# Columns of a weight used chunk by chunk: `w_val` laid out in four chunks of 128 output columns, and the steps of the program written in another order

## The chip, the cores and the metric

The kernel runs on one core of one Trainium2 chip. The metric is device microseconds (us) of one execution, as the median of several runs. One further execution was profiled, and the views below come from it.

TensorE (PE) does the matmuls, VectorE (DVE), ScalarE (ACT) and GpSimd (POOL) the elementwise work, and SyncE (SP) issues the DMAs. PEld is TensorE's loading of weights.

## The reference, cut to what matters

```python
B, H, S, Ns, D = 8, 8, 512, 32, 64              # all float32
scores = x @ state.T / sqrt(D)                  # per batch and head: [512, 32]
xread  = softmax(scores) @ state                # tokens read the state
scores2 = state @ x.T / sqrt(D)
sread  = softmax(scores2) @ x                   # the state reads the tokens
y = concat([xread, sread], axis=2)              # [B, H, 544, 64] -> x: [B, 544, 512]

gate = sigmoid(causal convolution of x over tokens, 5 taps, one weight per channel)
val  = x @ w_val                                # 512 x 512
out  = (gate * val) @ w_out                     # 512 x 512, out: [8, 544, 512]
```

Since `xread` is a product of probabilities and the state, `xread @ w_val` is computed as probabilities times (`state @ w_val`). The 512 token rows of each batch go through the batch loop; the 32 state rows of all batches are gathered and done once, in a tail.

## The kernel before, in words

**The work of a batch.** Eight batches, and per batch a chain: `load_xT` and `load_x` fetch the tokens; `scores` (tile `sc`) multiplies them with the scaled state `ss`; the softmax over the state runs as `mx` (maximum), `sl` (scores less maximum), `ex` (exponential), `sm` (sum, then a small number is added by `guard`), `rc` (its reciprocal), `ex` times `rc`, and the transposes by `probs` into `a`; the softmax over the tokens runs as `nb`, `e2`, `sum2`, `r2`, and the transposed exponentials (`e2p`, copied to `e2T`) multiply `x` in `state_read` (`srp`), whose result goes by `sr` and the transpose `srT` to the tail's rows. `state_val` multiplies the state with `w_val` (`sgv`); a scaling writes it as `sw0` for batch 0 and as `swh` with a rest `swl` for the others. `read` gives `xr`, the gate's taps follow (`acc`, `last`), and `sig` is the gate. `values` (`val`) multiplies `a` with the scaled `sgv`: two matmuls of plain f32 for each of four column chunks of batch 0, six matmuls of split numbers for the others. `gated` gives `g`, which is split into `gh` and `gl`, `project` (`op`) multiplies by `w_out` in twelve matmuls for each of four token tiles, and `o` is stored.

**Batch 0 is done otherwise in two ways.** Its scores and its first softmax are done in two halves of the tokens, as `xT` comes in two loads; and its taps are folded into the read: `z5` is the state times the five taps (`tap_state`, on POOL), and `read_conv` accumulates five shifted reads in `xr`, so that `gate_read` (L528) makes `sig` of `xr` directly.

**The weights.** `w_val` and `w_out` reach the core as 64-bit numbers, each 128 rows of 512 (one chunk, 512 KB) in one load (`vw`, `ow`). A chunk is turned into f32 by four steps: `wc` on ScalarE (L305), its clamp on POOL or VectorE (L320), `wp` on ScalarE (L313) or VectorE, and the join on VectorE (L325), which for `w_val` writes its part of `wv`. Chunks are rows of `w_val`, that is input channels, and `state_val` sums over nothing else: each of the eight matmuls of `state_val` takes 64 of the 512 input channels and all 512 output columns.

**What sets the order.** The program is a list of numbered steps; the string `ORDER` names them one by one in the order in which they are written out, with a letter where a step may run on several engines (`a`, `v`, `g`). Each engine runs its own steps in that order. `PLACES` says which buffer or PSUM bank (`ps0` to `ps7`) each tile takes; a tile that takes the place of another waits until the last reader of that one is done, so a load can be held at SyncE by the buffer that it writes to. `warm_up(i)` is a pair of matmuls whose result nobody reads.

The matmuls that the change divides, as they stand before:

```python
def state_val(b):
    for q in range(SB):
        for g in range(NG):
            h = slice(D * g, D * g + D)
            nc.tensor.matmul(
                get("sgv", b, g)[NS * q:NS * q + NS], su[h, b, q], wv[h, q],
                start=True, stop=True, tile_position=(D * g, NS * q))
```

Of the kernel before, what the change touches and what calls it, by code (L numbers as in the profile page):

```python
# [833 lines left out]
```

## Time and profile before

| | |
|---|---|
| time, median of 3 runs | 214.68 us (214.29 to 215.73) |
| the profiled execution's own time | 213.62 us |
| its span (first to last instruction) | 211.8 us |
| instructions | 4629 |
| TensorE busy | 204.5 us, 97% of the span |
| VectorE, ScalarE, POOL busy | 172.6, 145.2, 148.7 us |
| bytes moved by DMA | 31.25 MB, 148 GB/s over the span |

The span is the profiled part of that execution; its own time holds some 1.8 us more. An engine counts as busy while it executes, and matmuls are pipelined, so a busy TensorE can still be waiting inside. The times in the rows count from the start of the span.

### The profile page before, as it was taken

How to read it: one execution, taken by the hardware profiler on the slowest of the kernel's cores; microseconds unless marked ns; L12 is line 12 of the kernel's file. 1: busy time of each engine (PE TensorE's matmuls, PEld its weight loads, DVE VectorE, ACT ScalarE, POOL GpSimd, SP SyncE). 2: the span in 40 equal slices, each digit the busy share in tenths (PEclk: the TensorE clock that was granted, in tenths of full speed). 3: DMA queues.
4: the chain of work that ended last, by engine and by line, in shares of the span. 5: the costliest groups of instructions: out<-in, count | busy, mean ns of one | idle time of the engine just before them, and what ended most of it. 6: DMA issues, size and time to landing. Idle time of an engine off the chain costs nothing.

```text
span 211.8 us, 4629 instructions
## 1 busy us (share of the span) xinstructions
PE 204.5 (97%) x1791; PEld 149.1 (70%) x1791; DVE 172.6 (81%) x269; ACT 145.2 (69%) x307; POOL 148.7 (70%) x128
## 2 busy tenths in 40 slices
PE   8977999999999999999999999999999999999994
PEld 8754344877588577877686858688866868898883
DVE  1699898999899998999889999969987896697300
ACT  2497999985995889879947983685666573642421
POOL 1179899879989996879987899795859914520200
PEclk9999999999999999999999999999999999999999
DMA  6999970000446885410009960209400400040316
GB/s 167 403 391 377 422 329 6 0 0 3 124 200 226 297 295 162 189 54 0 3 2 325 388 280 3 99 0 288 161 0 3 152 3 0 0 150 3 149 50 198
DMA packets 9364, 31.25 MB, mean 148 GB/s; under 512 B 1130, under 2 KB 1406, under 8 KB 7422
## 3 DMA queue, kind: packets, MB, share of 16 engines
q1 hardware_dynamic: 9342, 30.96, 40.1%
q8 instruction: 14, 0.23, 0.4%
q14 instruction: 8, 0.07, 0.1%
HBM read 22.04 MB, written 8.91 MB: 146 GB/s over the span
## 4 chain that ended last, share of the span: by engine, by line
PE 88%; DVE 3%; POOL 3%; DMA 2%; ACT 1%; issue 0%; SPq 0%; DVEq 0%; POOLq 0%
PE val L560 20%; PE op L568 14%; PE op L569 14%; PE op L570 14%; PE srp L414 4%; PE sgv L369 4%; PE xr L497 3%; PE e2p L404 3%; PE sc L386 3%; PE tval L633 3%; DMA su<-sT 2%; PE xr L512 2%; POOL ex L269 1%; PE top L569 1%; PE top L568 1%; PE top L570 1%
## 5 line engine op out<-in xcount | busy, mean ns | idle before, releaser
L537 DVE SCALAR_TENSOR_TENSOR acc<-xr,cw,acc 128x511 f32<-128x511 f32 (+2 forms) x84 | 59.8, 737 | 4.5 <-ACT last L264 2.2
L568 PE MATMUL op<-woh,gh 128*128 128x512 f32 (+1 forms) x132 | 52.2, 396 | 0.0
L569 PE MATMUL op<-wol,gh 128*128 128x512 f32 (+1 forms) x132 | 51.2, 388 | 0.0
L570 PE MATMUL op<-woh,gl 128*128 128x512 f32 (+1 forms) x132 | 51.0, 387 | 0.0
L269 POOL TENSOR_TENSOR acc<-acc,last 128x508 f32<-128x508 f32 x24 | 31.2, 1301 | 17.3 <-DVE acc L537 11.5
L269 POOL TENSOR_TENSOR gl<-g,gh 128x512 fp32r<-128x512 f32 x28 | 36.9, 1326 | 8.4 <-ACT gh L256 7.5
L568 PEld LDWEIGHTS op<-woh,gh 128*128 128x128 f32 x132 | 24.9, 189 | 6.2 <-ACT o L256 0.8
L570 PEld LDWEIGHTS op<-woh,gl 128*128 128x128 f32 x132 | 24.8, 188 | 5.5
L569 PEld LDWEIGHTS op<-wol,gh 128*128 128x128 f32 x132 | 24.8, 188 | 4.9
L563 DVE SCALAR_TENSOR_TENSOR g<-sig,val 128x512 f32<-128x512 f32 x32 | 21.6, 682 | 7.1 <-PE val L560 3.4
L256 ACT COPY o<-op 128x512 f32<-128x512 f32 (+1 forms) x32 | 18.0, 575 | 10.0 <-PE op L570 8.4
L549 ACT ACTIVATE sig<-acc 128x512 f32<-128x512 f32 x28 | 17.5, 640 | 8.6 <-POOL acc L269 7.9
L532 ACT ACTIVATE acc<-xr,cw 128x512 f32<-128x512 f32 x28 | 19.5, 699 | 5.6 <-PE xr L497 4.2
L560 PE MATMUL val<-ah,swh 128*128 128x512 f32 x56 | 23.1, 412 | 0.0
L560 PE MATMUL val<-ah,swl 128*128 128x512 f32 x56 | 22.1, 394 | 0.0
L560 PE MATMUL val<-al,swh 128*128 128x512 f32 x56 | 22.0, 392 | 0.0
L264 ACT ACTIVATE last<-xr,cw 128x508 f32<-128x508 f32 x23 | 16.0, 696 | 4.8 <-DVE acc L537 3.5
L269 POOL TENSOR_TENSOR sl<-sl,mx 128x1024 f32<-128x1024 f32 (+1 forms) x8 | 14.5, 1811 | 5.1 <-DVE mx L460 5.0
L269 POOL TENSOR_TENSOR al<-sl,ah 128x1024 fp32r<-128x1024 f32 x7 | 16.8, 2399 | 1.5 <-ACT ah L256 1.4
L256 ACT CAST gh<-g 128x512 fp32r<-128x512 f32 x21 | 12.9, 628 | 6.5 <-DVE g L563 6.5
L269 POOL TENSOR_TENSOR ex<-ex,rc 128x1024 f32<-128x1024 f32 (+1 forms) x9 | 15.6, 1728 | 0.4 <-DVE rc L477 0.4
L560 PEld LDWEIGHTS val<-ah,swh 128*128 128x128 f32 x56 | 10.5, 188 | 4.6 <-issue 1.6
(126 smaller groups left out, 389.6 us busy)
## 6 DMA issues: line engine op xcount, KB each, us to landing
x<-x SPq DMA_DIRECT2D x8, 1024.0 KB, 8.6
out<-o SPq DMA_DIRECT2D x31, 256.0 KB, 2.5
xT<-xT SPq DMA_DIRECT2D x7, 1024.0 KB, 5.9
vw<-w_val SPq DMA_DIRECT2D x4, 512.0 KB, 7.2
ow<-w_out SPq DMA_DIRECT2D x4, 512.0 KB, 7.3
xT<-xT SPq DMA_DIRECT2D x2, 512.0 KB, 5.1
su<-sT SPq DMA_DIRECT2D x2, 256.0 KB, 3.8
z<-z SPq DMA_DIRECT2D x2, 256.0 KB, 7.4
```

The lines of the kernel that those rows point to most:

```text
L256: nc.scalar.copy(out, in_)
L264: nc.scalar.mul(out, in_, factor)
L269: (nc.vector if e == "DVE" else nc.gpsimd).tensor_tensor(out, a, b, op=how)
L369: nc.tensor.matmul(get("sgv", b, g)[NS * q:NS * q + NS], su[h, b, q], wv[h, q], start=True, stop=True, tile_position=(D * g, NS * q))
L532: nc.scalar.mul(get("acc", b, pr), pt, cw[:, HALO, pr:pr + 1])
L537: nc.vector.scalar_tensor_tensor(acc[:, d:], get("xr", b, pr)[:, :S - d], cw[:, HALO - d, pr:pr + 1], acc[:, d:], op0=ALU.mult, op1=ALU.add)
L549: nc.scalar.activation(get("sig", b, pr), get("acc", b, pr), AF.Tanh, scale=0.5)
L560: nc.tensor.matmul(get("val", b, k), w, a, start=(i == 0), stop=(i == len(parts) - 1))
L563: nc.vector.scalar_tensor_tensor(get("g", b, k), get("sig", b, k), 1.0, get("val", b, k), op0=ALU.add, op1=ALU.mult)
L568: nc.tensor.matmul(pt, gh, woh[:, k, c], start=(k == 0), stop=False)
L569: nc.tensor.matmul(pt, gh, wol[:, k, c], start=False, stop=False)
L570: nc.tensor.matmul(pt, gl, woh[:, k, c], start=False, stop=(k == NPR - 1))
```

## The change

`w_val` is laid out on the host so that a chunk of 128 rows in memory holds all 512 input channels of 128 output columns. `wv` becomes `[128, chunk, input block, 128]`. `state_val` of batches 1 to 7 reads all chunks with one matmul as before, through another view; that of batch 0 is divided into four parts, `state_val_part(0, k)`, of eight matmuls with 128 columns, and each part has two scalings `state_val_part_high`, of 128 columns each, in place of two of 512. The tail's use of `wv` follows the new shape.

`ORDER` and `PLACES` are replaced as a whole. Of the loads, the state (`su`) and the taps (`cww`) come first, then both halves of batch 0's tokens; which engine does a clamp, a copy, an addition or a split differs in many steps of all batches.

```diff
-        ("ident", [P, P], F32), ("wv", [P, NPR, C], F32), ...
+        ("ident", [P, P], F32), ("wv", [P, NPR, NPR, P], F32), ...
...
+    def columns(k):
+        return wv[:, k].rearrange("p q c -> p (q c)")
+
+    def state_val_part(b, k):
+        for q in range(SB):
+            for g in range(NG):
+                h = slice(D * g, D * g + D)
+                nc.tensor.matmul(
+                    get("sgv", b, g, k)[NS * q:NS * q + NS, :P], su[h, b, q], wv[h, k, q],
+                    start=True, stop=True, tile_position=(D * g, NS * q))
+
+    def state_val_part_high(e, b, g, k):
+        scale(e, get("sw0", b)[:, g, k * P:(k + 1) * P], get("sgv", b, g, k)[:, :P], HALF)
+
     def state_val(b):
...
-                    get("sgv", b, g)[NS * q:NS * q + NS], su[h, b, q], wv[h, q],
+                    get("sgv", b, g)[NS * q:NS * q + NS].rearrange("p (k c) -> p k c", c=P), su[h, b, q], wv[h, :, q],
...
-        op(state_val, b)
-        for g in range(NG):
-            op(state_val_high, b, g)
-            if b > 0:
+        if b > 0:
+            op(state_val, b)
+            for g in range(NG):
+                op(state_val_high, b, g)
                 op(state_val_low, b, g)
+        else:
+            for k in range(NPR):
+                op(state_val_part, b, k)
+                for g in range(NG):
+                    op(state_val_part_high, b, g, k)
...
-    weights(w_val, "vw", "v", lambda k: wv[:, k])
+    weights(w_val, "vw", "v", columns)
...
-        "w_val": np.ascontiguousarray(moe_w_val).view(np.int64),
+        "w_val": np.ascontiguousarray(moe_w_val.reshape(NJ, P, NJ, P).transpose(2, 1, 0, 3)).view(np.int64).reshape(moe_w_val.shape),
```

Two places show how the order moves. A row names the line, the operation and the tiles; `sgv_0_1_3` is the second half (1) of batch 0's (0) part 3. Lines are those of each kernel's own file, so that L369 before answers to L374 and L385 after, and L512 to L528.

VectorE and POOL ahead of batch 0's read. POOL before:

```order
L320 TENSOR_SCALAR wc_v_2_181<-wc_v_2_181 128x512
L320 TENSOR_SCALAR wc_v_3_184<-wc_v_3_184 128x512
L269 TENSOR_TENSOR ex_0_168<-ex_0_168,rc_0_191 128x2x256
L425 TENSOR_SCALAR sm_0_175<-sm_0_175 128x2x8
L269 TENSOR_TENSOR ex_0_168<-ex_0_168,rc_0_191 128x2x256
L269 TENSOR_TENSOR z5_0_260<-z_72,cwb_71 128x640
L320 TENSOR_SCALAR wc_v_1_245<-wc_v_1_245 128x512
```

POOL after:

```order
L322 TENSOR_SCALAR wc_v_1_181<-wc_v_1_181 128x512
L271 TENSOR_TENSOR ex_0_179<-ex_0_179,rc_0_192 128x2x256
L441 TENSOR_SCALAR sm_0_183<-sm_0_183 128x2x8
L271 TENSOR_TENSOR z5_0_261<-z_72,cwb_71 128x640
L271 TENSOR_TENSOR ex_0_179<-ex_0_179,rc_0_192 128x2x256
L322 TENSOR_SCALAR wc_v_3_257<-wc_v_3_257 128x512
L322 TENSOR_SCALAR wc_o_0_259<-wc_o_0_259 128x512
```

`z5` has moved ahead of the second half of `ex`.

VectorE at the same place, before:

```order
L470 TENSOR_REDUCE sm_0_175<-ex_0_168 128x2x8
L325 SCALAR_TENSOR_TENSOR wv_65<-wc_v_3_184,wp_v_3_195 128x512
L477 RECIPROCAL rc_0_191<-sm_0_175 128x2x8
L488 STREAM_TRANSPOSE a0_0_239<-ex_0_168 128x256
L449 STREAM_TRANSPOSE sl_1_242<-sc_1_1_221 128x512
L449 STREAM_TRANSPOSE sl_1_242<-sc_1_0_219 128x512
L488 STREAM_TRANSPOSE a0_0_239<-ex_0_168 128x256 x3
L460 TENSOR_REDUCE mx_1_328<-sl_1_242 128x32
```

and after:

```order
L327 SCALAR_TENSOR_TENSOR wv_65<-wc_v_1_181,wp_v_1_185 128x512
L486 TENSOR_REDUCE sm_0_183<-ex_0_179 128x2x8
L465 STREAM_TRANSPOSE sl_1_221<-sc_1_1_210 128x512
L465 STREAM_TRANSPOSE sl_1_221<-sc_1_0_208 128x512
L493 RECIPROCAL rc_0_192<-sm_0_183 128x2x8
L504 STREAM_TRANSPOSE a0_0_250<-ex_0_179 128x256 x2
L476 TENSOR_REDUCE mx_1_253<-sl_1_221 128x32
L504 STREAM_TRANSPOSE a0_0_250<-ex_0_179 128x256 x2
```

The maximum of batch 1, `mx_1`, which followed all transposes of `a0`, now stands ahead of the last two.

ScalarE behind the copy of `e2T_0_0`, up to the gate's `sig_0_0`, before:

```order
L305 ACTIVATE wc_o_2_326<-ow0_2_151 128x512
L313 ACTIVATE wp_o_2_334<-ow0_2_151,ones_69 128x512
L305 ACTIVATE wc_v_0_338<-vw0_0_230 128x512
L313 ACTIVATE wp_v_0_348<-vw0_0_230,ones_69 128x512
L467 ACTIVATE ex_1_350<-sl_1_242 128x1024
L397 ACTIVATE e2_1_0_366,sum2_1_367<-sc_1_0_219,nb_1_336 128x512
L528 ACTIVATE sig_0_1_371<-xr_0_1_284 128x512
L421 ACTIVATE r2_0_374<-sum2_0_200,ones_69 128x2
L264 ACTIVATE sw0_0_386<-sgv_0_1_355 128x512
L305 ACTIVATE wc_o_1_390<-ow1_1_202 128x512
L305 ACTIVATE wc_o_3_397<-ow1_3_269 128x512
L528 ACTIVATE sig_0_0_401<-xr_0_0_282 128x512
```

and after:

```order
L266 ACTIVATE sw0_0_277<-sgv_0_1_1_242 128x128
L315 ACTIVATE wp_o_0_339<-ow0_0_236,ones_69 128x512
L307 ACTIVATE wc_v_0_341<-vw0_0_263 128x512
L315 ACTIVATE wp_v_0_343<-vw0_0_263,ones_69 128x512
L483 ACTIVATE ex_1_345<-sl_1_221 128x1024
L315 ACTIVATE wp_o_1_349<-ow1_1_266,ones_69 128x512
L307 ACTIVATE wc_o_1_351<-ow1_1_266 128x512
L307 ACTIVATE wc_v_2_366<-vw0_2_364 128x512
L544 ACTIVATE sig_0_3_374<-xr_0_3_300 128x512
L315 ACTIVATE wp_v_2_379<-vw0_2_364,ones_69 128x512
L544 ACTIVATE sig_0_0_385<-xr_0_0_294 128x512
```

A scaling of part 1 (`sgv_0_1_1`) stands early; the other (`sgv_0_0_1`) is three rows further up. `wc_v_2`, `sig_0_3` and `wp_v_2` now stand between `wc_o_1` and `sig_0_0`, where there were the batch's second scaling and `wc_o`.

On TensorE, `state_val(0)` as a whole stood between `xr` and `val` before. Now its part 1 stands ahead of `xr`, and `val_0_1` follows `xr` at once; then come part 3, `state_val(1)` (`sgv_1`), part 0, `val_0_3`, `val_0_0` and the scores of batch 2, and part 2 only behind these.

SyncE's loads of weights and tokens behind the first ones, before:

```order
L296 DMA ow0_2_151<-w_out 128x512
L296 DMA ow1_1_202<-w_out 128x512
L296 DMA vw0_0_230<-w_val 128x512
L277 DMA xT_2_237<-xT 128x2048
L296 DMA ow1_3_269<-w_out 128x512
L274 DMA x_0_276<-x 128x2048
L296 DMA ow0_0_340<-w_out 128x512
```

and after:

```order
L298 DMA vw0_0_263<-w_val 128x512
L298 DMA ow1_1_266<-w_out 128x512
L298 DMA ow1_3_353<-w_out 128x512
L298 DMA vw0_2_364<-w_val 128x512
L276 DMA x_0_382<-x 128x2048
L279 DMA xT_2_437<-xT 128x2048
```

Chunk 2 of `w_val` (`vw0_2`), which was the fifth load of the program, has become one of the last of the weights, ahead of `x_0` and `xT_2`.

## Rows read from the trace of the kernel before

**Rows 1.** The page: busy time of TensorE as a whole, and the granted clock of TensorE in 40 equal slices of the span, in tenths of full speed (9 is 90% or more).

```profile
PE 204.5 (97%) x1791; PEld 149.1 (70%) x1791; DVE 172.6 (81%) x269; ACT 145.2 (69%) x307; POOL 148.7 (70%) x128
PEclk9999999999999999999999999999999999999999
```

**Rows 2.** The waits of TensorE: the waiting line, the operation that ended the wait, us in total, how many, the longest.

```profile
PE sc L386 <- DMA xT<-xT: 1.2, 1, 1.2
...
PE srT L439 <- ACT sr L436: 0.4, 1, 0.4
```

**Rows 3.** Stretches of the span: from and to, length, then the busy time (and instructions) of TensorE, its weight loads, VectorE, ScalarE and POOL, the granted clock, the DMA engines' busy share and GB/s.

```profile
18.14:22.61 4.47, 4.47 (x81) 1.70 (x81) 4.12 (x8) 3.42 (x5) 4.47 (x5) 1.00 0.99 391
22.61:41.44 18.83, 18.76 (x199) 9.42 (x191) 17.57 (x27) 17.60 (x39) 17.21 (x18) 1.00 0.44 181
41.44:160.00 118.56, 118.56 (x1090) 86.08 (x1089) 109.46 (x165) 88.94 (x193) 101.12 (x75) 1.00 0.39 139
160.00:180.00 20.00, 19.56 (x147) 15.48 (x146) 15.79 (x22) 12.54 (x29) 12.02 (x10) 1.00 0.11 41
```

**Rows 4.** The timeline of TensorE up to 31 us: start, duration, engine, line, operation, output and inputs, how many records, and in brackets the idle time before with what ended it.

```profile
1.03 5.36 PE L340 MATMUL warm<-cwb 128*128 128x128 f32 x32 [1.03 <-DVE cwb L335]
6.56 0.67 PE L386 MATMUL sc<-xT,ss 64*32 64x256 f32 x16 [0.16 <-POOL ss L290]
...
9.40 2.50 PE L340 MATMUL warm<-ident 128*128 128x128 f32 x20
13.10 1.09 PE L386 MATMUL sc<-xT,ss 64*32 64x512 f32 x16 [1.20 <-DMA xT<-xT]
...
15.44 1.04 PE L404 MATMUL e2p<-ident,e 128*128 128x128 f32 x8
...
18.14 4.54 PE L512 MATMUL xr<-a,z 32*64 32x512 f32 x80 [1.22 <-POOL z L269]
...
24.63 3.67 PE L560 MATMUL val<-a,sw 128*128 128x512 f32 x8
28.23 1.10 PE L414 MATMUL srp<-x,e2T 128*32 128x64 f32 x64
29.26 1.09 PE L369 MATMUL sgv<-wv,su 64*32 64x512 f32 x16
30.28 1.12 PE L560 MATMUL val<-a,sw 128*128 128x512 f32 x2
```

**Rows 5.** The timeline of POOL and VectorE ahead of batch 0's read, in the same columns (`z` is the tile `z5`, `a` the tile `a0`).

```profile
14.80 0.26 POOL L425 TENSOR_SCALAR sm<-sm 128x16 f32<-128x16 f32 x1
15.10 0.25 DVE L477 RECIPROCAL rc<-sm 128x16 f32<-128x16 f32 x1
15.51 1.05 POOL L269 TENSOR_TENSOR ex<-ex,rc 128x512 f32<-128x512 f32 x1 [0.44 <-DVE rc L477]
15.58 1.26 DVE L449 STREAM_TRANSPOSE sl<-sc 128x512 f32<-128x512 f32 x2
16.52 1.57 POOL L269 TENSOR_TENSOR z<-z,cwb 128x640 f32<-128x640 f32 x1
16.77 1.05 DVE L488 STREAM_TRANSPOSE a<-ex 128x256 f32<-128x256 f32 x3
17.75 1.18 DVE L460 TENSOR_REDUCE mx<-sl 128x32 f32<-128x1024 f32 x1
```

**Rows 6.** The timeline of ScalarE from 14 to 27 us, in the same columns.

```profile
14.14 0.25 ACT L256 COPY cwb<-cwbp 128x128 f32<-128x128 f32 x1
...
14.97 0.67 ACT L305 ACTIVATE wc_v<-vw 128x512 f32<-128x512 f32 x1
15.54 0.74 ACT L313 ACTIVATE wp_v<-vw,ones 128x512 int32<-128x512 uint8 x1
16.20 1.07 ACT L256 COPY e2T<-e2p 128x512 f32<-128x512 f32 x2
17.14 0.70 ACT L305 ACTIVATE wc_o<-ow 128x512 f32<-128x512 f32 x1
...
21.16 1.06 ACT L467 ACTIVATE ex<-sl 128x1024 f32<-128x1024 f32 x1
22.12 0.67 ACT L397 ACTIVATE e<-sc,nb 128x512 f32<-128x512 f32 x1
...
23.83 0.60 ACT L264 ACTIVATE sw<-sgv 128x512 f32<-128x512 f32 x1 [0.27 <-PE sgv L369]
...
25.44 1.09 ACT L528 ACTIVATE sig<-xr 128x512 f32<-128x512 f32 x2
26.56 0.74 ACT L313 ACTIVATE wp_o<-ow,ones 128x512 int32<-128x512 uint8 x1
```

**Rows 7.** DMA issues: output and input, queue, operation, how many, KB each, us from issue to landing. In this order they were issued at 0.72, 3.41, 5.15, 14.00 and 74.39 us.

```profile
xT<-xT SPq DMA_DIRECT2D x1, 512.0 KB, 4.4
xT<-xT SPq DMA_DIRECT2D x1, 1024.0 KB, 9.6
z<-z SPq DMA_DIRECT2D x1, 256.0 KB, 9.7
vw<-w_val SPq DMA_DIRECT2D x1, 512.0 KB, 5.6
xT<-xT SPq DMA_DIRECT2D x1, 1024.0 KB, 4.9
```

More of the change, by code (lines that the diff above doesn't have):

```diff
@@ new lines @@
+e2T2 e2T_1_1 e2T_2_1 e2T_3_1 e2T_6_1
+g0 wc_conv wc_v_1 wc_o_0 wc_o_1 g_0_1 g_0_3 g_1_0 g_1_2 g_2_3 g_3_0 g_3_1 g_4_0 g_4_2 g_5_1 g_5_3 g_6_0 g_6_3
+g0 g_7_0 g_7_2 tg_0
+g1 wc_v_0 wc_v_2 wc_v_3 wc_o_2 wc_o_3 g_0_0 g_0_2 g_1_1 g_1_3 g_2_0 g_2_1 g_2_2 g_3_2 g_3_3 g_4_1 g_4_3 g_5_0
+g1 g_5_2 g_6_1 g_6_2 g_7_1 g_7_3 tg_1
+gh0 gh_0_1 gh_1_0 gh_2_2 gh_3_3 gh_4_3 gh_5_1 gh_6_1 gh_7_3
+gh1 gh_0_0 gh_2_0 gh_4_2 gh_6_2 tgh_0
+gh2 gh_0_3 gh_2_3 gh_4_1 gh_6_3 tgh_1
+gh3 gh_0_2 gh_2_1 gh_4_0 gh_6_0
+gh4 gh_1_3 gh_3_0 gh_5_2 gh_7_1
@@ new lines @@
+ps1 warm_1 sc_0_0 xr_0_1 op_0_1 sgv_1_1 xr_1_2 op_1_1 xr_2_3 op_2_1 op_2_3 op_3_3 sc_4_0 e2p_4_0 xr_4_1 xr_5_0
+ps1 xr_6_3 op_6_1 e2p_7_0 xr_7_3 op_7_0_0 warm_14 warm_16
+ps2 warm_2 wp_v_0 wp_v_3 wp_o_3 sc_0_1 sgv_0_0_0 val_0_1 op_0_0 op_0_2 op_1_2 sc_2_1 sgv_2_0 val_2_2 sgv_3_1
+ps2 val_3_1 op_3_0 val_4_0 val_4_2 op_4_0 sc_5_1 sgv_5_0 val_5_2 op_5_2 srp_6 sgv_6_1 val_6_0 val_6_1 val_6_2
+ps2 val_7_3 op_7_3
+ps3 warm_3 cwbp_0 sgv_0_0_2 val_0_2 sc_1_0 val_1_0 val_1_3 op_1_3 val_2_3 xr_3_3 srT_4 xr_4_0 op_4_2 srT_5 xr_5_2
@@ new lines @@
+ps3 val_5_0 sgv_6_0 op_6_2 xr_7_1 val_7_1 op_7_2 warm_11
+ps4 warm_4 wp_o_0 wp_o_1 wp_o_2 srp_0 srT_0 sgv_0_1_1 sgv_0_0_3 halo_0_1 e2p_1_0 e2p_1_1 val_1_2 srp_2 sgv_2_1
+ps4 xr_2_0 op_2_2 e2p_3_1 sc_4_1 sgv_4_0 srp_5 op_5_3 sc_6_0 op_6_3 sc_7_1 xr_7_0 tval_1 warm_13
+ps5 warm_5 wp_v_1 wp_v_2 e2p_0_0 xr_0_3 srp_1 sgv_1_0 val_1_1 sc_2_0 srT_2 xr_2_2 op_2_0 e2p_3_0 srT_3 xr_3_2
+ps5 val_3_0 val_3_2 e2p_4_1 val_4_3 op_4_3 e2p_5_0 e2p_5_1 sc_6_1 xr_6_1 xr_7_2 op_7_1
+ps6 warm_6 cwbp_1 sgv_0_0_1 xr_0_2 halo_0_2 op_0_3 xr_1_1 e2p_2_1 xr_2_1 srp_3 op_3_1 xr_4_2 val_4_1 sc_5_0
@@ L140 @@
 sm1 sm_1 sm_3 sm_5 sm_7
-sum20 sum2_0 sum2_2 sum2_5
+sum20 sum2_0 sum2_4 sum2_6
 sum21 sum2_1 sum2_7
-sum22 sum2_3
-sum23 sum2_4 sum2_6
+sum22 sum2_2 sum2_5
+sum23 sum2_3
 swh0 sw0_0 swh_2 swh_4 swh_6
 swh1 swh_1 swh_3 swh_5 swh_7
-swl0 vw1_3 ow1_1 swl_1 swl_3 swl_5 swl_7
-swl1 vw1_1 ow1_3 swl_2 swl_4 swl_6
-x0 x_0 x_3 x_6
-x1 x_1 x_4 wvh
-x2 x_2 x_5 x_7 wvl
-xT0 xT_0 xT_2 xT_4 xT_6
-xT1 xT_1 xT_3 xT_5 xT_7
+swl0 vw1_1 ow1_1 swl_1 swl_3 swl_5 swl_7
+swl1 vw1_3 ow1_3 swl_2 swl_4 swl_6
+x0 x_0 x_4 x_7 wvl
+x1 x_1 x_3 x_5 x_6
+x2 x_2 wvh
+xT0 xT_0 xT_2 xT_4 xT_5 xT_7
+xT1 xT_1 xT_3 xT_6
 """
@@ L630, in tail_values @@
         xh, xl, wh, wl = tail_parts("xth"), tail_parts("xtl"), weight_parts("wvh"), weight_parts("wvl")
[L631 removed]
+        parts = [(w[:, k, i * P:(i + 1) * P], x[:, i]) for i in range(NPR) for w, x in ((wh, xh), (wh, xl), (wl, xh))]
         for i, (w, x) in enumerate(parts):
```

169 lines of the change are left out of this document (74 added, 95 removed).

## The prediction

> **What bounds the kernel now.** I read the busy times first, then what TensorE waited for, then the stretches in which it waited. TensorE is busy in 97% of the span and its granted clock stands at full speed, the upper of its two levels (2.4 GHz), in every slice [rows 1]. Its waits are few: 1.2 us for `xT`, 0.4 us for the transpose `srT` of batch 7 [rows 2], which is the 0.44 missing in 160 to 180 [rows 3], and 1.22 us for the first matmul of batch 0's read (`xr`), which waits for POOL's `z5` [rows 4]. By stretch, from 18.14 us to the last matmul there is next to no idle time: 4.47 of 4.47, 18.76 of 18.83, 118.56 of 118.56, 19.56 of 20.00 [rows 3]. So the kernel is a preparation of 18.14 us, whose matmuls are mostly warm-up, and behind it a column of TensorE work without holes. The time after is the time before, plus how much later that column begins, plus what is added to it, plus the holes that it gets. The second thing to see is ScalarE: in 22.61 to 41.44 it is busy 17.60 of 18.83 us [rows 3], so there it has nothing to give.
>
> The profiled execution took 213.62 us, 1.82 more than its span of 211.8, and lies 1.06 under the median of 214.68. I work in the span and add the difference to the median.
>
> **What the split does.** In the old program `state_val(0)` needs all of `w_val`; in the new one a part needs one chunk. Only part 1 stands ahead of `xr`. `state_val(1)`, which needs all four chunks, stands between part 3 and part 0, so parts 0 and 2 gain nothing from being separate. Removed: 8 matmuls of 512 columns (16 records); the same group of batch 1 took 1.02 us (29.26 to 30.28) [rows 4]. Added: 32 of 128 columns, three quarters of them behind the start of `xr`. A group of 256 columns takes 0.67 against 1.09 for 512 [rows 4], so the time falls by less than half when the columns are halved; on that line 128 columns cost 0.46 (0.67 less half of 0.42), and by columns alone a quarter of 1.02, 0.26. I take 0.40: three parts are 1.2 us for 1.02, **+0.2** (-0.25 to +0.35). The eight scalings that replace two cost some 0.25 each by the copy of 128 columns (`cwb`) against 0.60 [rows 6]; six of them are on ScalarE, +0.9 us of work there, which is in the walk below.
>
> **The start of `xr`.** `xT_1` has the same 3348 KB to land up to its end in both orders, so it lands at 13.0 as before [rows 7]. VectorE's sum of the second half of batch 0's exponentials stands behind one `w_val` join in both, so POOL's guard `sm` comes as before at about 14.8 to 15.06 [rows 5]. Before, POOL then did `ex` (1.05) and `z5` (1.57), and `xr` began at 18.14 behind `z5`, with VectorE's transposes done at 17.82. Now POOL does `z5` first: 15.0 + 1.57 + 1.05 = 17.6, and the last two transposes of `a0` still have to follow. On VectorE `mx_1` (1.18) stands ahead of them. Ahead of it are `sl_1`'s two transposes (1.26, from the end of batch 1's scores at 14.2), `rc` (0.25) and two transposes of `a0` (0.7), so it starts at 16.6, handovers included, and ends at 17.8. Two transposes at 0.35 (1.05 for three) [rows 5] end at 18.5, so `xr` starts at 18.6: **+0.45** (+0.2 to +0.7).
>
> **Does the column stay full?** This is where the time is decided. TensorE finishes `xr` (4.47) at 23.07 and `val_0_1` (3.60 for two such, so 1.80) at 24.9 [rows 4]. Next is part 3. Its second PSUM bank was `xr_0_0`'s, so it waits until ScalarE has read that in `sig_0_0`. I walk ScalarE from `e2T_0_1`, with the distances from start to start in [rows 6] (0.57 a `wc`, 0.66 a `wp`, 0.47 an `e2T` copy, 0.96 `ex_1`, 0.56 a `sig`). The scores of batch 1 end at 14.2; one warm-up step (four records at 0.125, 0.5) and four transposes (half of the 1.04 for eight) follow [rows 4], so `e2T_0_1` starts at 15.3. Then `e2T`, `wc_v_3` (its 4116 KB land at 14.8, as `z` did [rows 7]), `wc_o_0`, `wp_v_3`, a scaling, `e2T`, a scaling, `wp_o_0`: 0.47 + 0.57 + 0.57 + 0.66 + 0.25 + 0.47 + 0.25 + 0.66 = 3.9, that is 19.2, with handovers 19.4. Then `wc_v_0`, `wp_v_0`, `ex_1`, `wp_o_1`, `wc_o_1`: 3.4, that is 22.8.
>
> Here the new wait bites. The load of `w_val`'s chunk 2 writes into the buffer of `w_out`'s chunk 0, so SyncE holds it until `wp_o_0` is done, 19.4; queued behind it are `x_0`, `xT_2`, `xT_3`. `x_0`'s consumer `srp_0` stands 8 us further on and covers it. How long 512 KB take on a nearly empty queue the trace shows once, at the start: 4.4. A load of 1024 KB at 74.4 us took 4.9, and at the 391 GB/s of 18.14 to 22.61 [rows 3] half of it is 1.3, so 3.6. Behind a queue 512 KB took 5.6 [rows 7]. Ahead of it is only `ow` chunk 3, issued 1.7 us earlier. I take 3.7, nearest to the late and empty queue: it lands at 23.2, and ScalarE, free at 22.8, waits 0.4. Then `wc_v_2`, `sig_0_3`, `wp_v_2`, `sig_0_0`: 0.57 + 0.56 + 0.66 + 0.55 = 2.3, with handovers 2.5, so part 3 can go on at 25.7 where TensorE came at 24.9: **0.8 us** of idle time (0 to 2.7: if ScalarE is 0.8 early, or the load takes 5.6). `state_val(1)` then waits 0.1 for `sig_0_1`, `val_0_3` 0.1 for the scalings, `srp_0` 0.2 for an `e2T` copy behind the same ScalarE queue: **+0.4** (0 to 0.8). In a sentence that the sum does without: the Trainium skill, "DMA: Bandwidth & Descriptors", section "Anatomy of one DMA — SWDGE (gpsimd) path", fits 2.0 us + bytes/436 GB/s for another queue than this one; by that the load takes an estimated 3.2, ScalarE waits for nothing, and my total would be 0.4 lower; the 4.4 at the start speaks against it.
>
> **The rest of the program** is reordered too. TensorE had no hole in 41.44 to 160 [rows 3], so nothing can be won there; a new hole of the size of that old one costs 0.44, and I allow two (0 to +0.9) and take none, because VectorE, ScalarE and POOL keep 9, 30 and 17 us free in those 118.56 [rows 3]. The old hole in 160 to 180 comes from a ScalarE queue that is now another; I take 0.3 of its 0.44 back: **-0.3** (-0.44 to 0). The warm-ups are 15 steps for 16 and lie ahead of `xr` in idle time, at no cost while the clock holds.
>
> **Sum.** 0.45 + 0.2 + 0.8 + 0.4 - 0.3 = +1.55: span 213.35, a profiled execution of 215.2, median 214.68 + 1.55 = **216.2**. That is 0.7%; a difference of under 1% is about what a measurement of this kernel can tell from no change.
>
> **Rivals.** *(1) Chunk 2 is later than I think.* If its load takes the 5.6 of the row with a queue ahead, it lands at 25.0, everything from `wc_v_2` on moves by 1.8, and TensorE's hole becomes 2.6: 218.0. For it: the only row at this age of the program is that one. Against: little is queued by then. Chance 0.15. *(2) The clock falls.* Between the last warm-up ahead of `xT_1` (three steps where the old kernel has five from 9.40 on, so up to 10.9) and 13.0 TensorE has nothing to do for 2.1 us, where the old kernel's longest such hole was 1.2 [rows 4]; its clock held. If it drops to 1.2 GHz, the price is about what the start paid for the low level: 5.36 us for 32 records against 0.125 each, 1.4 us [rows 4], so 217.6. This rule speaks against the change: the Trainium skill, "TensorE: Matmul & The Clock Gate", section "Why this matters for your kernels", warns of idle gaps between bursts of matmuls; no row here shows a gap of this size in mid-program. Chance 0.07. *(3) ScalarE keeps ahead, so that the time doesn't rise.* One mechanism: if ScalarE reaches `sig_0_0`'s end by 24.9 (0.8 earlier than I walk it, with chunk 2 landed by 22.4), the holes of 0.8 and 0.4 vanish, parts that cost the 0.26 of their columns save 0.25, and the old 0.44 is gone: 0.45 - 0.25 - 0.44 = -0.25, 214.4; an `xr` that starts as before makes it 214.0. For it: each of ScalarE's steps in the walk has a small handover in it that I guessed. Against: 0.8 us in nine steps is a lot, and ScalarE's row shows it full. Chance 0.23. *(4) The split does not do what it says*: for parts 0 and 2 that is so by the order, and it is in the forecast.
>
> **How the numbers follow.** Forecast (215.3 to 217.1) 0.55, rival 1 (217.1 to 218.8) 0.15, rival 2 (216.8 to 219) 0.07, rival 3 (213.4 to 215.3) 0.23. Slower by over 1% is above 216.83: rivals 1 and 2 and a fifth of the forecast, 0.32. Faster by over 1% is under 212.5, which would take a column that begins 2 us earlier, and POOL's chain forbids it: 0.06. Between: 0.62. The range leaves a tenth out above, at 218.4, and a tenth below; below it would end at 214.2, and I carry it on to 213.6 for a `xr` that isn't later.
>
> **What the changed profile would show.** Right: the first `xr` at 18.4 to 18.8, with its wait ended by VectorE's `a`, not by POOL's `z`; a wait of TensorE of 0.6 to 1.2 at `sgv` near 25, ended by ScalarE's `sig`; ScalarE without idle time from 15.3 to 22.8 and then a short wait for `vw`; no hole between 160 and 180. Wrong: `xr` at or before 18.1, no wait at `sgv`, granted clock under 1 anywhere before the last matmul, or holes behind 41 us that together exceed 1 us.

## The result, and the profile after

Over 20 runs each, the changed kernel takes 216.19 us (215.13 to 217.50) and the old one 214.25 (213.51 to 215.73): a ratio of 1.0091, 95% interval 1.0077 to 1.0105, some 1.9 us slower. The profiled execution of the changed kernel has a span of 213.8 us, the old one's 211.8. In 7 of its 20 runs, the profiled one among them, the mean granted clock was 0.989 to 0.992; the median of these 7 is 216.42, that of the other 13, at 0.998 and more, is 216.01, and the two groups overlap (215.62 to 217.50 and 215.13 to 216.69).

The page of the changed kernel, in the form of [rows 1], and the stretches of its span, in the form of [rows 3]:

```profile
PE 206.8 (97%) x1835; PEld 151.9 (71%) x1835; DVE 169.6 (79%) x271; ACT 146.2 (68%) x311; POOL 147.7 (69%) x128
PEclk9988999999999999999999999999999999999999
```

```profile
14.46:17.87 3.41, 3.41 (x29) 2.70 (x30) 3.41 (x8) 2.38 (x7) 2.94 (x4) 0.50 0.92 371
...
19.26:41.44 22.18, 21.81 (x278) 12.41 (x278) 18.54 (x30) 21.17 (x47) 21.64 (x21) 1.00 0.52 203
41.44:160.00 118.56, 118.56 (x1020) 85.98 (x1019) 105.68 (x159) 89.88 (x194) 101.02 (x77) 1.00 0.42 145
160.00:182.00 22.00, 22.00 (x240) 16.27 (x239) 16.78 (x28) 13.70 (x31) 11.46 (x10) 1.00 0.04 14
```

The share of TensorE is the same 97%, and again nothing is idle behind 41 us; the old hole in 160 to 180 is gone. From 14.46 to 17.87 us the granted clock is half. ScalarE is busy 21.17 of 22.18 us from the first `xr` to 41.44, and POOL 21.64.

The timeline of TensorE in the changed kernel (columns as in [rows 4]):

```profile
1.03 5.34 PE L342 MATMUL warm<-cwb 128*128 128x128 f32 x32 [1.03 <-DVE cwb L337]
6.58 0.67 PE L402 MATMUL sc<-xT,ss 64*32 64x256 f32 x16 [0.21 <-DMA xT<-xT]
...
9.34 1.60 PE L342 MATMUL warm<-ident 128*128 128x128 f32 x12
13.32 1.09 PE L402 MATMUL sc<-xT,ss 64*32 64x512 f32 x16 [2.38 <-POOL sl L271]
...
15.28 1.06 PE L420 MATMUL e2p<-ident,e 128*128 128x128 f32 x4
...
17.79 1.54 PE L342 MATMUL warm<-ident 128*128 128x128 f32 x12
19.26 4.71 PE L528 MATMUL xr<-a,z 32*64 32x512 f32 x80
23.90 1.98 PE L576 MATMUL val<-a,sw 128*128 128x512 f32 x4
25.81 0.40 PE L374 MATMUL sgv<-wv,su 64*32 64x128 f32 x2
26.58 0.45 PE L374 MATMUL sgv<-wv,su 64*32 64x128 f32 x14 [0.37 <-ACT sig L544]
26.96 1.20 PE L385 MATMUL sgv<-wv,su 64*32 64x512 f32 x16
27.81 0.56 PE L374 MATMUL sgv<-wv,su 64*32 64x128 f32 x16
```

`xr` begins at 19.26, 1.12 later than before, right behind the warm-ups, and part 3 of `state_val(0)` (25.81) stops after its first matmul for 0.7 us. Between the earlier warm-ups, which end at 10.94, and the scores at 13.32 TensorE is idle for 2.38 us. The profile names POOL's `sl`, which the scores don't read; the load of `xT` issued at 3.41 landed 9.8 us later, at 13.2. `e2p` takes 1.06 for four transposes; in [rows 4] eight took 1.04.

ScalarE, POOL and VectorE of the changed kernel in the same stretch:

```profile
16.38 0.59 ACT L258 COPY e2T<-e2p 128x512 f32<-128x512 f32 x1 [1.03 <-PE e2p L420]
...
24.10 0.67 ACT L307 ACTIVATE wc_v<-vw 128x512 f32<-128x512 f32 x1 [0.29 <-DMA vw<-w_val]
...
25.96 1.06 ACT L544 ACTIVATE sig<-xr 128x512 f32<-128x512 f32 x2
```

```profile
10.98 1.18 POOL L292 TENSOR_SCALAR ss<-su 128x384 f32<-128x384 f32 x1
12.13 1.05 POOL L271 TENSOR_TENSOR sl<-sl,mx 128x512 f32<-128x512 f32 x1
...
15.28 0.27 POOL L441 TENSOR_SCALAR sm<-sm 128x16 f32<-128x16 f32 x1 [0.39 <-DVE sm L486]
15.63 1.54 POOL L271 TENSOR_TENSOR z<-z,cwb 128x640 f32<-128x640 f32 x1
```

```profile
13.91 0.69 DVE L327 SCALAR_TENSOR_TENSOR wv<-wc_v,wp_v 128x512 int32<-128x512 int32 x1 [0.82 <-POOL wc_v L322]
...
18.21 0.77 DVE L504 STREAM_TRANSPOSE a<-ex 128x256 f32<-128x256 f32 x2
```

ScalarE waits 0.29 for chunk 2 at 24.10, and ends `sig_0_0`, the first of the two at 25.96, where part 3 goes on. On POOL the scaled state of batches 1 to 3 (10.98, 1.18 us) stands ahead of the second half of `sl`, which begins at 12.13. In the old trace ScalarE scales the state, and POOL's second half of `sl` begins 1.1 us earlier:

```profile
11.03 1.05 POOL L269 TENSOR_TENSOR sl<-sl,mx 128x512 f32<-128x512 f32 x1 [4.17 <-DVE mx L460]
```

Behind `sl` stands POOL's clamp of a `w_val` chunk, for which VectorE's join waits 0.82 us (13.91), and behind that join the sum that `sm` needs.

**Where the 2 us were lost.** The read of batch 2 in TensorE's timeline, of the old kernel and of the new:

```profile
55.48 1.19 PE L497 MATMUL xr<-sl,z 32*64 32x512 f32 x16
```

```profile
54.15 1.11 PE L513 MATMUL xr<-sl,z 32*64 32x512 f32 x16
```

It starts at 55.48 us in the old trace and at 54.15 in the new; but the new program has left one projection (`op_0_0`, 2.87) and one group of `e2p` (0.44) for later, so it stands at 57.46 in terms of the old order, 1.98 late. From there to the start of the last matmul (208.52 and 210.48) the old kernel needs 153.04 us, and the new one, without these two, 153.02. All of the loss is made ahead of batch 2's read: 1.12 by the start of `xr`, and the rest behind it. The three late parts take 1.98 us, 0.7 of it the wait, where the whole of `state_val(0)` took 0.88 from its start to the next step's in the old trace; that is 1.1 more, of which other steps give back 0.24.

```profile
22.61 1.09 PE L369 MATMUL sgv<-wv,su 64*32 64x512 f32 x16
23.49 1.06 PE L386 MATMUL sc<-xT,ss 64*32 64x512 f32 x16
```

### The profile page after: what moved, and what is told of

Its sections match the earlier page's. It is cut to its first block, busy times and chain, and to the rows that moved or that the text cites. A ratio compares the mean times of both kernels' runs of the same rounds, so it can differ in the third digit from the quotient of the medians.

```text
span 213.8 us, 4725 instructions
## 1 busy us (share of the span) xinstructions
PE 206.8 (97%) x1835; PEld 151.9 (71%) x1835; DVE 169.6 (79%) x271; ACT 146.2 (68%) x311; POOL 147.7 (69%) x128
## 4 chain that ended last, share of the span: by engine, by line
PE 88%; DMA 5%; ACT 3%; POOL 1%; SPq 1%; issue 1%; ACTq 0%
PE val L576 21%; PE op L584 14%; PE op L586 14%; PE op L585 14%; PE srp L430 4%; PE xr L513 3%; PE e2p L420 3%; PE sc L402 3%; DMA ow<-w_out 3%; PE sgv L385 3%; PE tval L649 3%; DMA vw<-w_val 2%; PE top L584 1%; PE top L585 1%; PE top L586 1%; ACT wc_v L307 1%
## 5 line engine op out<-in xcount | busy, mean ns | idle before, releaser
L553 DVE SCALAR_TENSOR_TENSOR acc<-xr,cw,acc 128x510 f32<-128x510 f32 (+2 forms) x84 | 60.9, 739 | 5.3 <-ACT last L266 2.0
L271 POOL TENSOR_TENSOR acc<-acc,last 128x508 f32<-128x508 f32 x26 | 33.3, 1287 | 14.8 <-DVE acc L553 13.2
L271 POOL TENSOR_TENSOR gl<-g,gh 128x512 fp32r<-128x512 f32 x27 | 34.8, 1294 | 3.4 <-ACT gh L258 3.0
L258 ACT COPY o<-op 128x512 f32<-128x512 f32 (+1 forms) x30 | 17.2, 579 | 15.1 <-PE op L586 14.4
L258 ACT CAST gh<-g 128x512 fp32r<-128x512 f32 x26 | 16.1, 627 | 7.3 <-DVE g L579 6.7
L271 POOL TENSOR_TENSOR sl<-sl,mx 128x1024 f32<-128x1024 f32 (+1 forms) x9 | 15.5, 1726 | 6.1 <-DVE mx L476 6.1
L266 ACT ACTIVATE last<-xr,cw 128x508 f32<-128x508 f32 x24 | 16.5, 697 | 2.1 <-POOL acc L271 1.7
```

Source lines behind the costliest of these rows:

```text
L258: nc.scalar.copy(out, in_)
L266: nc.scalar.mul(out, in_, factor)
L271: (nc.vector if e == "DVE" else nc.gpsimd).tensor_tensor(out, a, b, op=how)
L553: nc.vector.scalar_tensor_tensor(acc[:, d:], get("xr", b, pr)[:, :S - d], cw[:, HALO - d, pr:pr + 1], acc[:, d:], op0=ALU.mult, op1=ALU.add)
```

## Experiments

Each kernel was run 6 to 12 times. A ratio is to the old kernel, run beside it. The numbers in the diffs are those of `ORDER`; beside them is what the step does.

**The clock.** *e1: two more warm-up steps in the changed kernel.*

```diff
-861 862 863 175        (warm_up 10 to 12, scores of batch 1)
+861 862 863 868 869 175
```

> The changed kernel with two more warm-up steps ahead of batch 1's scores (five, as in the old kernel, where the change left three); nothing else differs. Theory A, the clock costs time: the changed kernel waits 2.4 us with nothing to do ahead of these scores and its granted clock is halved from 14.5 to 17.9 us. With the hole at 1.4 us the clock stays at full speed; the transposes e2p take 0.5 us a group instead of 1.1, ScalarE's copy e2T starts at about 15.4 instead of 16.4, the load of w_val's chunk 2 is issued about 0.9 earlier, xr starts at about 19.05 (held by VectorE's transposes, no longer by the warm-ups) and part 3 finds its bank free. Time 0.7 to 1.0 us less than the changed kernel, 215.2 to 215.5 where that has 216.2. Theory B, the order of VectorE and POOL and the load of chunk 2 set everything: the clock stays up but xr gains only 0.2 and the wait at part 3 stays; time 0.2 less. Theory C: other idle time, not this hole, halved the clock, and it falls all the same; no change.

Measured: 216.17 us, ratio 1.0081 (1.0054 to 1.0108), no different from the changed kernel. The hole is 0.96 us, the clock stays at full speed, `e2p` takes 0.60. TensorE's timeline in e1, and ScalarE's when it comes to chunk 2:

```profile
1.03 6.08 PE L342 MATMUL warm<-cwb 128*128 128x128 f32 x32 [1.03 <-DVE cwb L337]
7.04 0.66 PE L402 MATMUL sc<-xT,ss 64*32 64x256 f32 x16
...
13.57 1.09 PE L402 MATMUL sc<-xT,ss 64*32 64x512 f32 x16 [0.96 <-POOL sl L271]
...
15.14 0.60 PE L420 MATMUL e2p<-ident,e 128*128 128x128 f32 x4
...
19.43 4.54 PE L528 MATMUL xr<-a,z 32*64 32x512 f32 x80 [1.38 <-DVE a L504]
...
26.06 0.40 PE L374 MATMUL sgv<-wv,su 64*32 64x128 f32 x2 [0.18 <-DVE ws_o L327]
27.13 0.45 PE L374 MATMUL sgv<-wv,su 64*32 64x128 f32 x14 [0.67 <-ACT sig L544]
```

```profile
24.63 0.69 ACT L307 ACTIVATE wc_v<-vw 128x512 f32<-128x512 f32 x1 [0.78 <-DMA vw<-w_val]
```

`xr` waits for VectorE's `a`, as theory A said, but starts no earlier: the first scores of this execution came 0.46 us later than in that of the changed kernel (7.04 for 6.58), right behind the 32 warm-up records at the start, which took 6.08 us here and 5.34 there. ScalarE comes to chunk 2 earlier and waits longer for it: issued at 19.81 (20.37 before), it landed 4.7 us later. Theory A falls as an account of the 2 us: with the clock up the median is the same. The two groups of runs above differ by 0.4 us in their medians and overlap, so they give no sure price of the fall.

*e2: two warm-up steps fewer in the old kernel.*

```diff
-852 853 854 855 856 166   (warm_up 10 to 14, scores of batch 1)
+852 853 854 166
```

> The old kernel with two of the five warm-up steps ahead of batch 1's scores taken away; nothing else differs. Theory A: the hole ahead of these scores grows from 1.2 to 2.2 us and the granted clock is halved for some 3.4 us behind it. xr is held by POOL and starts at 18.1 to 18.4 as before, but the e2p transposes take 0.5 us longer a group, so ScalarE's weight conversions come 0.5 to 1.0 us later and state_val waits for them: 0.4 to 1.0 us slower than the old kernel, 214.7 to 215.3 where that has 214.25. Theory C: a hole of this size does not matter, clock 1.00 throughout, time unchanged.

Measured: 214.56 us, ratio 1.0005 (0.9986 to 1.0024). The hole was 1.68 us in the profiled execution and not the 2.2 that were meant, since the 32 warm-up records at the start took 6.74 us in it (5.36 in [rows 4]); the granted clock stayed at 1.00 there. In 3 of the 12 runs the mean was 0.991 or 0.992, in the others 0.997 and more. The time doesn't show it, but a hole as long as that of the changed kernel was not made.

*e12: the changed kernel with one warm-up step of the three.*

```diff
-861 862 863 175
+861 175
```

> The changed kernel with two of its three warm-up steps ahead of batch 1's scores taken away, so that TensorE waits some 3.4 us there. If the clock's fall costs what the runs of the changed kernel say (those in which it fell took 0.5 us more), the clock falls in every run now and the median is 0.2 to 0.5 us above the changed kernel's 216.2. If its fall costs nothing, the time is unchanged. If 3.4 us of idle time cost more than 2.4, over 1 us above.

Measured: 217.44 us, ratio 1.0156 (1.0125 to 1.0187), 1.25 above the changed kernel. Its timeline of TensorE, and the stretch from the scores on (columns as in [rows 3]):

```profile
14.43 1.96 PE L402 MATMUL sc<-xT,ss 64*32 64x512 f32 x16 [3.46 <-POOL sl L271]
```

```profile
14.43:17.50 3.07, 3.07 (x21) 1.41 (x22) 2.30 (x4) 2.03 (x6) 2.60 (x4) 0.50 1.01 410
```

The scores themselves now run at the lower level, 1.96 us for 1.09. From 11.88 to 18.71 us the granted clock averages 0.52, and its mean over the whole execution is 0.984 in all six runs. So the longer fall goes with a loss that the shorter one of the changed kernel doesn't show. How much of the loss is the clock's is not separated: in the profiled execution the load of `xT` that these scores read took 10.9 us for 9.8, which alone makes 1.1 us of the hole.

**The split by itself.** *e4: the old order with the new layout alone. e3: the same, and `state_val(0)` in four parts at its old place.*

The edit that divides it, in e3:

```diff
+        if b == 0:
+            for k in range(NPR):
+                for q in range(SB):
+                    for g in range(NG):
...
+                            get("sgv", b, g)[NS * q:NS * q + NS, k * P:(k + 1) * P], su[h, b, q], wv[h, k, q],
```

> The old order and the undivided state_val, with the new layout of w_val alone: chunks are output columns, and each matmul of state_val reads its 512 columns as four pieces of 128. Theory A: the pieces cost nothing, matmuls of state_val take 1.0 us a batch as before and the time is that of the old kernel within 0.2 us. Theory B: the pieces slow the 64 matmuls of state_val, 0.1 to 0.3 us a batch, 0.8 to 2 us in all, which would be the column's unexplained 0.8 us in the changed kernel.

> The old order with the new layout of w_val, and batch 0's state_val done in four parts of eight matmuls with 128 columns, all at the old place and into the old two tiles, with the two old scalings. The price of small matmuls alone. Theory A (each part costs 0.35 to 0.5 us, as parts 0 and 3 do in the changed kernel): four parts take 1.4 to 2.0 us for 0.9 to 1.0, so the time rises by 0.4 to 1.0 us. Theory B (the columns alone count): four parts take 1.0 us and the time is unchanged.

Measured: e4 214.31 us, ratio 0.9999 (0.9981 to 1.0017); e3 214.43, ratio 1.0009 (0.9991 to 1.0027). The timeline of TensorE in e3:

```profile
23.27 1.16 PE L374 MATMUL sgv<-wv,su 64*32 64x128 f32 x64
24.17 1.12 PE L398 MATMUL sc<-xT,ss 64*32 64x512 f32 x16
```

The 64 records of 128 columns take 0.90 us to the next step (23.27 to 24.17) where 16 of 512 took 0.88. Theory A for e4 and theory B for e3: the layout costs nothing, nor do small matmuls that follow each other. In the changed kernel part 0 takes 0.49 (27.81 to 28.30) and part 2 0.35, not a quarter of 0.9 each. A good share of that is only where one step ends and the next begins: the steps ahead of them came out shorter, 0.85 for `state_val(1)` and 0.89 for the scores of batch 2, where 16 records of 512 columns took 1.02 in [rows 4]. That a part costs more because it stands alone is a reading that no run tests; nor was the new order run with `state_val(0)` undivided. So what e3 and e4 show is that in the old order the split is free, and that the loss comes with the new order.

**The start and chunk 2.** *e5: e1 with the old order of VectorE and POOL ahead of `xr`. e7: e1 with chunk 2 loaded early, into the buffer `ah1`. e8: both. e6: both, and `wp_o_1` on VectorE.*

```diff
 e5
-104g 179 176 105 ... 98 99 182 ... 131g ... 106g ... 108 107
+104g 105 98 106g 179 176 ... 131g ... 108 107 99 182   (rc, a0, POOL's ex ahead of sl_1, z5 and mx_1)
 e7
-65 ... 40           (loads of w_out's chunk 3, w_val's chunk 2)
+40 65
 e6
-58a
+58v
```

> e1_warm5 with the old kernel's order of VectorE and POOL ahead of xr: rc and one transpose of a0 ahead of the transposes of sl_1, the other three transposes ahead of mx_1, and POOL's ex ahead of z5. Theory A (the column is as late as its start): xr starts at about 18.8 where e1_warm5 has 19.43, and the time falls by 0.5 to 0.6 us against e1_warm5, to about 215.6. Theory B (chunk 2 of w_val, which state_val(1) needs, is what counts: loaded late, converted by ScalarE behind sig_0_3): xr starts earlier by 0.6 us, TensorE's wait at part 3 or at state_val(1) grows by the same 0.6 us, and the time is that of e1_warm5, 216.2, within 0.2 us.

> e1_warm5 with chunk 2 of w_val loaded some 7 us earlier, into a buffer that is free until batch 1 needs it, ahead of w_out's chunk 3 in SyncE's order. Theory B: ScalarE no longer waits for the chunk (0.78 us in e1_warm5), wp_v_2 then follows sig_0_3 at once, state_val(1) starts 0.6 to 0.9 us earlier, the wait at part 3 falls from 0.85 us to under 0.3 us; time 0.5 to 0.9 us less than e1_warm5, about 215.4. Theory A: the wait at part 3 is made by ScalarE's own queue, and goes on as before; time within 0.2 us of e1_warm5.

> e5_start_order and e7_chunk2_early together. Theory B with ScalarE behind it: xr starts 0.6 us earlier and chunk 2 is there, but wp_v_2 and sig_0_0 still end when ScalarE gets there, so most of the start's gain turns into a wait at part 3; 0.0 to 0.4 us less than e7_chunk2_early. If start and chunk 2 were independent costs, their gains would add: 1.1 to 1.5 us less than e1_warm5, about 214.8.

> e8_both with one of the eight conversions in this stretch (wp_o_1, 0.73 us on ScalarE) done by VectorE, as in the old kernel; VectorE has 1.5 us free there. If ScalarE's queue is the last bound at part 3, the time falls by a further 0.4 to 0.7 us against e8_both, to the old kernel's 214.1 to 214.6. If not, it is that of e8_both.

Measured: e5 215.91 us, ratio 1.0090 (1.0057 to 1.0123); e7 215.80, 1.0078 (1.0055 to 1.0101); e8 216.18, 1.0091 (1.0063 to 1.0119); e6 215.75, 1.0078 (1.0051 to 1.0104). All four lie within 0.4 us of e1, inside their intervals. TensorE in e7 and in e8:

```profile
19.68 4.54 PE L528 MATMUL xr<-a,z 32*64 32x512 f32 x80 [1.37 <-DVE a L504]
...
26.31 0.61 PE L374 MATMUL sgv<-wv,su 64*32 64x128 f32 x16 [0.17 <-DVE ws_o L327]
26.99 1.09 PE L385 MATMUL sgv<-wv,su 64*32 64x512 f32 x16
```

```profile
18.77 4.54 PE L528 MATMUL xr<-a,z 32*64 32x512 f32 x80 [0.94 <-POOL z L271]
...
26.29 0.59 PE L374 MATMUL sgv<-wv,su 64*32 64x128 f32 x16 [1.07 <-DVE ws_o L327]
26.98 1.09 PE L385 MATMUL sgv<-wv,su 64*32 64x512 f32 x16
```

`xr` begins 0.91 earlier in e8 (0.40 of it because the first scores of that execution came at 7.08 for 7.48), and `state_val(1)` at the same 26.98: the gain is a wait at part 3, 1.07 us, ended by VectorE's join of `w_out`'s chunk 1. `wp_o_1` holds the PSUM bank of part 3's first half until that join. In VectorE's order the join stands behind the reciprocal `rc` of batch 1, which waits for POOL's `sm`; VectorE in e8:

```profile
24.75 0.35 DVE L493 RECIPROCAL rc<-sm 128x32 f32<-128x32 f32 x1 [0.56 <-POOL sm L441]
...
25.56 0.67 DVE L327 SCALAR_TENSOR_TENSOR ws_o<-wc_o,wp_o 128x512 int32<-128x512 int32 x1
```

e5 waits the same 1.07 us there: this was its theory B, but what ends the wait is another step than it named. In e7 the wait for chunk 2 is gone and the join takes its place; its 0.4 us are less than its theory B wanted and inside the noise. e6, with a conversion less on ScalarE, still waits 1.03 us at part 3 for the same join, so ScalarE's queue was not the last bound.

**All waits behind `xr`, and the start.** *e9: e6 with POOL's two splits of `w_out` behind `ex` of batch 1, and the join ahead of `rc`. e10: e9 with the scaled state on ScalarE and `wp_o_0` on VectorE. e11: e10 with `e2T_0_0` and part 1's scalings earlier on ScalarE, and the clamp of `w_out`'s chunk 3 earlier on POOL.*

```diff
 e9
-185 74g 70g 186g 187 41 180 149 57g 142 59 42g 43a 188g 80 44 133
+185 41 57g 59 42g 186g 187 180 149 142 43a 44 188g 133 74g 70g 80
 e10
-15g ... 53a
+15a ... 53v         (state_scale 1 3 behind the copy 27a)
 e11
-46 ... 111 ... 123a 112a ... 124a ... 75g ... 152g 66 ... 67g
+46 111 112a 123a 124a ... 66 67g 75g 152g
```

> e6_both_dve with POOL's two splits of w_out (woh, 2.04 us) moved behind ex of batch 1, so that POOL's clamps of w_out's chunk 1 and w_val's chunk 2 stand ahead of them, and VectorE's join of w_out's chunk 1 ahead of rc of batch 1. Theory D: three waits end within a microsecond of each other behind val_0_1: part 3's first bank (wp_o_1, read by VectorE's join, which waits for POOL), its second bank (ScalarE's sig_0_0) and state_val(1) (the join of w_val's chunk 2); taking one or two of them away shows the third. With all three, part 3 starts 0.4 to 0.6 us earlier after the start of xr, state_val(1) 0.7 to 0.9, and the time falls by 0.5 to 0.9 us against e6_both_dve, to about 215.0. Theory E, the later program gives back whatever is won here: time as e6_both_dve within 0.2 us.

> e9_three_waits with the scaled state of batches 1 to 3 (ss, 1.18 us on POOL between the two halves of batch 0's scores) on ScalarE in an idle stretch, as in the old kernel, and wp_o_0 on VectorE. Theory D: the chain POOL, ScalarE, VectorE ahead of xr is 0.7 to 1.0 us shorter, xr starts at 17.8 to 18.2 as in the old kernel or before it, and with the waits behind it small the time comes back to that of the old kernel, 214.0 to 214.6. Theory E: no change against e9_three_waits.

> e10_early_start with two moves. On ScalarE the copy of e2T_0_0 and the scalings of part 1 stand directly behind wc_v_3: the copy empties the PSUM bank that xr_0_3 takes, and in e10_early_start it ended at 19.1 us, 1 us behind the start of xr. On POOL the clamp of w_out's chunk 3 stands ahead of the first rest of w_out: its late join held a bank of the scores of batch 2 for 1.1 us. Theory D (each later start and each wait is one bank or one buffer, and all of them in series): xr runs without a stop from 18.1 to 22.7, the scores of batch 2 without one from 31, and the time falls by 1.2 to 2.0 us against e10_early_start, to 214.6 to 215.4. Theory E (something else in the new order keeps the column late): under 0.5 us.

Measured: e9 217.17 us, ratio 1.0136 (1.0104 to 1.0168), 1.4 slower than e6, a miss for both theories. e10 216.61, 1.0105 (1.0078 to 1.0132). e11 216.31, 1.0097 (1.0069 to 1.0124). In e9 part 3 starts at 25.14 and goes on at 25.80, as early behind `xr` as forecast, but `state_val(1)` waits 0.49 us for the join of `w_val`'s chunk 2 and comes only 0.2 earlier behind `xr` than in e6, and then TensorE does this:

```profile
32.05 1.04 PE L402 MATMUL sc<-xT,ss 64*32 64x512 f32 x2
33.27 0.66 PE L402 MATMUL sc<-xT,ss 64*32 64x512 f32 x7 [0.18 <-DVE ws_o L327]
```

The scores of batch 2 stop after two records for a bank that the join of `w_out`'s chunk 3 frees, behind a clamp that POOL now does later. In e10 `xr` starts at 18.14, the old time, and takes 5.57 us for 4.54, because its last bank is emptied by ScalarE's copy of `e2T_0_0`; here TensorE's steps and its weight loads:

```profile
18.14 5.57 PE L528 MATMUL xr<-a,z 32*64 32x512 f32 x80
```

```profile
19.19 0.23 PEld L528 LDWEIGHTS xr<-a,z 32*64 32x64 f32 x15 [0.28 <-ACT e2T L258]
```

In e11 both are mended (`xr` 4.66, the scores of batch 2 1.09), and two other steps wait instead: `state_val(1)` 0.48 us for the join of `w_val`'s chunk 2, and the read of batch 1 in the middle. A bank of that read is freed by a scaling of part 2 on VectorE, behind a reciprocal that waits for POOL (TensorE's steps, its weight loads, VectorE):

```profile
34.07 2.03 PE L513 MATMUL xr<-sl,z 32*64 32x512 f32 x16
```

```profile
34.99 0.22 PEld L513 LDWEIGHTS xr<-sl,z 32*64 32x64 f32 x10 [0.73 <-DVE sw L268]
```

```profile
34.59 0.17 DVE L447 RECIPROCAL r<-r 128x2 f32<-128x2 f32 x1 [0.79 <-POOL r L441]
34.67 0.27 DVE L268 TENSOR_SCALAR sw<-sgv 128x128 f32<-128x128 f32 x1
```

So theory D held for each wait that it named, and not for their sum. The 1.1 us won at the start of `xr` (18.11 for 19.26) come to nothing, as batch 2's read begins at 54.55 in e11 and at 54.15 in the changed kernel. From that read to the start of the last matmul every kernel with the new order takes 156.3 to 156.6 us, so whatever an order wins or loses lies ahead of it. By the time, theory E holds for e11, and for e10 within the noise (0.6 us under e9); e9 is slower than either theory had it. No kernel here beats the old one, and none of these orders brings its time back. The traces show how this comes about: each wait taken away shows the next, and behind three of them (the join of `w_out`'s chunk 1, that of its chunk 3, the reciprocal) stands POOL. That POOL is what bounds this stretch is my reading; no run gives it less work there.

## Why the prediction was right, and where it was not

Forecast were +1.55 us and 216.2; measured were +1.94 (216.19 less 214.25) and a median of 216.19. The direction holds, the rise was 0.39 too small, and the places of the three large terms hold. That the two medians agree to 0.01 us is luck: I started from the 214.68 of three runs, 0.43 above the 214.25 of twenty. Inside the sum, too, errors offset each other. By the traces it is 1.12 for the start, 0.4 for the parts and 0.7 for the wait, less 0.24 that other steps give back: 1.98. By its steps:

- **The start of `xr`, +0.45.** It was +1.12, beyond my +0.7. The step that failed is "POOL's guard `sm` comes as before": it came at 15.28 for 14.80. I looked at VectorE's order alone; the change had also put the scaled state of batches 1 to 3 on POOL (10.98, 1.18 us), between the halves of `sl`, and the second half began at 12.13 for 11.03. e10, which takes it away (and moves `wp_o_0`), has `xr` at 18.14 where e9 has 18.76. The transposes behind `mx_1` came as foreseen, and ended at 18.98; that `xr` starts at 19.26 and not there is the clock: the two groups of `e2p` take 1.06 and 1.11 us where e1 has 0.60 and 0.66, so the warm-ups behind them, no slower themselves (1.54 for 1.50), end late. My sign for `xr`, 18.4 to 18.8 with a wait ended by VectorE's `a`, did not come; that wait shows in e1.
- **Small parts, +0.2.** It was about +0.4. The three parts behind `xr` take 1.98 us in all, some 1.2 without the 0.7 of waiting, which is my 1.2; but what they replace took 0.88 and not the 1.02 that I took from batch 1's group. My way to the 1.2 does not hold either: where parts follow each other, in e3, they take 0.23 each, which is less than the 0.26 of my lower bound.
- **The wait at part 3, 0.8.** It was 0.7: the first matmul at 25.81, the next at 26.58. The load of chunk 2 took 3.6 us (3.7 forecast), ScalarE waited 0.29 for it (0.4), and `sig_0_0` ended the wait. By the fit of the Trainium skill ("DMA: Bandwidth & Descriptors", section "Anatomy of one DMA — SWDGE (gpsimd) path"), which is for another queue, the load would have taken an estimated 3.2 and ScalarE waited for nothing; the 3.6 here and the 4.7 of e1 lie above it, while the load just ahead of it, `w_out`'s chunk 3, took 3.2 in both traces. Every time in the walk came 0.9 late because `e2T_0_1` began at 16.38 and not 15.3, behind the slow `e2p` (15.78 in e1, with the clock up). TensorE came as much later, by POOL's delay and the late warm-ups; that the two delays were equal, so that the difference stayed, is luck. What I had not seen is that this was one of three waits of the same age: e7 removes chunk 2's, and the join of `w_out`'s chunk 1 holds part 3 instead.
- **Small waits behind it, +0.4.** `state_val(1)`, `val_0_3` and `srp_0` show no idle time worth naming; this term was too high.
- **The hole in 160 to 180, -0.3.** It is gone (22.00 of 22.00). But the stretch from batch 2's read on is no shorter, 153.02 for 153.04, so its 0.44 was given back in small pieces.
- **The rival of the clock, 0.07.** It happened, with its place (behind a hole of 2.4 us, I had 2.1), in 7 of 20 runs, the profiled one among them, so one of my signs of being wrong, a granted clock under 1, came true. Its price was not 1.4: the two groups of runs differ by 0.4, and e1 shows that the result does not hang on it. In e1 `xr` waits 1.38 us for VectorE, so the matmuls ahead of it, which run at the lower level in the changed kernel, had time to spare. I had taken the 1.4 from the warm-ups at the start, where the granted clock reads 1.00 [rows 1], so no row showed it as a price of the lower level. I gave the rival too small a chance, and it did not decide.
- **The rival without loss, 0.23.** It wanted ScalarE 0.8 us earlier. In e6 chunk 2 is there in time and ScalarE has a conversion less, and part 3 still waits 1.03 us; e8 and e11 show that even a start of `xr` 0.5 to 1.1 us earlier is not enough.

What stays open: which order of POOL would let an early start reach the end. I tried three; a queue busy 21.64 of 22.18 us has little room for it.

## What to carry to other kernels

Where four engines are near full, a step's price is not its own duration but the next thing due on the engine that it was put on: look for what the change adds to every queue ahead of the critical start, not only to the one that the diff is about. Before giving a wait a price, list all that must be ready at that point (the buffer, the PSUM bank, the operand, each by its last reader); if several fall within a microsecond, removing one wins little (under 0.6 us in each step here, and e9 lost 1.4). Splitting an operation frees its operands one by one, but only the parts that stand ahead of the first full user gain from it.
